# Handing out GpSimd's work on a group of first products two places later, in a kernel of top-k attention and a two-layer block

## The chip, the cores and the metric

The kernel runs on one core of one Trainium2 chip. The metric is the device time of one execution in microseconds; a median of several runs is given for each kernel, and one further execution was recorded by the profiler. The engines are named as in the profile: PE is TensorE, PEld its weight loads, DVE is VectorE, ACT is ScalarE, POOL is GpSimd, SP is SyncE, which issues the DMAs.

## The reference

Attention with the 32 largest scores of each row kept, for 8 batches, 8 heads, 576 positions, 64 values a head; its output is laid out as 4608 rows of 512 and goes through two matrix products with an activation between them.

```python
scores = scale * np.matmul(q, k.transpose(0, 1, 3, 2))
kth = np.partition(scores, -top_k, axis=-1)[..., -top_k:-top_k + 1]
scores = np.where(scores >= kth, scores, -1000000000.0)
attn = np.exp(scores - np.max(scores, axis=-1, keepdims=True))
attn = attn / (np.sum(attn, axis=-1, keepdims=True) + 1e-09)
x = np.matmul(attn, v)                       # (B,H,S,D) -> (B*S, H*D)
h = x @ w_in                                 # 4608 x 512 @ 512 x 2048
g = np.where(h >= 1, h, np.where(h <= -1, 0.0, (h + 1) ** 2 / 4))
out = g @ w_out                              # 2048 x 512
```

All inputs and outputs are 32-bit floats.

## The kernel before, in words

**Steps.** The attention is cut into 144 steps. A step is one tile of 128 rows of one batch for a pair of heads; the 64 rows left over of two batches are paired into steps of their own. The main loop (L744) has index m; each pass is cut into seven places (`SLOTS`, L767), and at each place the loop issues a part of several stages that belong to different steps:

- `scores` (L340): PE multiplies queries and keys (L358), ACT copies the products from PSUM to the tile s (L359). This runs two to three steps ahead.
- `first_top` and `weights` (L382, L417): DVE finds the 32nd largest score of each row. It folds each row into halves (L372, one instruction for the larger and one for the smaller of two elements), and then alternates between taking eight largest (L392, L420, L428, L439) and replacing them (L379); L446 and the scan L451 settle the threshold kth from two sorted lists. ACT makes the exponentials e (L395), and L458 on DVE masks e by the threshold and sums it into z. L372, L451 and L458 are DVE's instructions with two tensors from SBUF.
- `divide` (L402), called inside `weights` of the next step, at its place 0: DVE takes the reciprocal of z (L404), and GpSimd multiplies the two heads' e by it (L411, two instructions), followed by a tiny subtraction for a later check (L414). In the first steps and the last ones (`by_tensor`, L766) a diagonal matrix on PE does the multiplication instead.
- `move_w` (L484), at place 3: ACT copies e to 16-bit halves (L488), which go to DRAM and come back transposed through two DMAs of SP's queue.
- `values` (L498), every two steps: PE multiplies the transposed weights by v (L506), ACT copies the result into a column of xT (L519).

**The two products.** As soon as all heads of 128 rows (a chunk, 36 in all) are in xT, `mlp` (L530) puts this chunk's work on the list `pending`. The 2048 hidden columns are 16 blocks of 128, taken two at a time: a group. `hidden(x)` makes group x: 16 matmul instructions (L539) into a PSUM tile ph, then ACT reads ph twice, as relu of half the value plus a half into r (L543) and as relu of the value minus one into g (L550), and GpSimd does the rest in three instructions: it bounds r at 1 (L555), squares it (L556) and adds it to g (L557). `final(f)` multiplies one block of g by w_out into py (L562), and after 16 blocks ACT copies py to y (L565) and SP stores it. In the list, the two `final` of a group come four groups (`LAG`) behind its `hidden`. r has two buffers and g has eight. For the last chunk, groups are one block wide and DVE takes the place of GpSimd.

**What sets the order.** PE, DVE, ACT and POOL get their instructions in an order written out by hand (`manual_schedule`, L658): the order in which the Python code calls them is the order of each engine's queue. `advance` (L649), called at the end of each place, adds a share to `due` and takes work from `pending` while enough is due: a `hidden` of a group costs 8 units, a `final` 4, and a chunk has 128 units, so that a step is due some 32. `pe_time`, `dve_time` and `usable` are estimates that keep the work from being taken too early. At place 2 of even steps (L795) a `hidden` taken last is followed by further items until a `final` was taken. While the weights are being brought to their form for the products (`converted < n_pieces`, the first eight steps), conversion pieces (L141) use GpSimd too (L158); in this phase a fixed share is due.

So GpSimd's queue holds, in the order of the calls: three instructions for each group, wherever `hidden` was taken, and at place 0 of each step the division L411 (two) with L414.

Of the kernel before, what the change touches and what calls it, by code (L numbers as in the profile page):

```python
# [17 lines left out]
ALU = mybir.AluOpType  # L18
# [8 lines left out]
def kernel(  # L27
# [10 lines left out]
    nc = tc.nc  # L38
# [17 lines left out]
    GROUP = 2  # L56
# [51 lines left out]
    n_pieces = NK * DFF // WC + NF * DM // WC  # L108
# [12 lines left out]
    def needed(f, second):  # L121

        return (f // n_in) * (NK + n_in * n_out) + NK + (n_out * (f % n_in + 1) if second else 0)
# [53 lines left out]
    def run(ctx, paired):  # L177
# [112 lines left out]
        def finish_turns():  # L290
            while turns:
                turns.pop(0)()
# [235 lines left out]
            return [(i * TL, (i + 1) * TL, out[r0 + i * S + SM:r0 + (i + 1) * S, :]) for i in range(2)]  # L528

        def mlp(xT, rows, pool, last):  # L530
            gs, group = {}, 1 if last else GROUP
            py = []

            def hidden(x):
                ph = ps.tile([P, group, P], F32, name="ph", tag="ph", bufs=3)
                for i in range(group):
                    f = x * group + i
                    for kk in range(NK):
                        nc.tensor.matmul(ph[:, i], w_in[:, kk, f * P:(f + 1) * P], xT[:, kk],  # L539
                                         start=(kk == 0), stop=(kk == NK - 1))  # L540

                r = pool.tile([P, GROUP, P], F32, name="r", bufs=2)[:, 0:group]
                nc.scalar.activation(r, ph, AF.Relu, bias=half, scale=0.5 * unit)  # L543
                gs[x] = g = pool.tile([P, GROUP, P], F32, name="g", bufs=2 * LAG)[:, 0:group]
                if last:
                    nc.scalar.activation(g, ph, AF.Relu, bias=minus_half, scale=0.5 * unit)
                    nc.vector.scalar_tensor_tensor(out=r, in0=r, scalar=1.0, in1=r, op0=ALU.min, op1=ALU.mult)
                    nc.vector.tensor_tensor(out=g, in0=r, in1=g, op=ALU.add)
                    return
                nc.scalar.activation(g, ph, AF.Relu, bias=minus, scale=unit)  # L550
                if converted < n_pieces and x % 2:
                    nc.scalar.activation(r, r, AF.Square)
                    nc.gpsimd.tensor_scalar(r, r, 1.0, 0.0, ALU.min, ALU.max)
                else:
                    nc.gpsimd.tensor_scalar(r, r, 1.0, 0.0, ALU.min, ALU.max)  # L555
                    nc.gpsimd.tensor_tensor(out=r, in0=r, in1=r, op=ALU.mult)  # L556
                nc.gpsimd.tensor_tensor(out=g, in0=r, in1=g, op=ALU.add)  # L557

            def final(f):
                if f == 0:  # L560
                    py.append(ps.tile([P, DM], F32, name="py", tag="py", bufs=1))
                nc.tensor.matmul(py[0], gs[f // group][:, f % group], w_out[:, f, :], start=(f == 0), stop=(f == NF - 1))  # L562
                if f == NF - 1:
                    y = (late or words).tile([P, DM], F32, name="y", bufs=1)
                    nc.scalar.activation(y, py[0], AF.Copy, scale=unit)  # L565
                    for p0, p1, dst in rows:
                        nc.sync.dma_start(out=dst, in_=y[p0:p1])

            behind = []
            while pending and pending[-1][3]:
                behind.insert(0, pending.pop())
            for x in range(NF // group + LAG):
                if x < NF // group:
                    pending.append((NK * group, needed(x * group + group - 1, False), partial(hidden, x), False))
                if x < LAG:
                    for _ in range(min(GROUP + 1, len(behind))):
                        pending.append(behind.pop(0)[0:3] + (False,))
                else:  # L580
                    for f in range((x - LAG) * group, (x - LAG + 1) * group):
                        pending.append((DM // P, needed(f, True), partial(final, f), x >= NF // group))
# [14 lines left out]
        n = len(steps)  # L597
# [6 lines left out]
        pending = deque()  # L604
        total, spent = len(chunks) * (NK * NF + NF * DM // P), 0
        converted, inspected, due = 0, 0, 0.0

        begun, pipe = 0, deque()

# [39 lines left out]
        def advance(amount, until):  # L649

            nonlocal due, pe_time
            due = due + amount if pending else 0.0
            pe_time = max(pe_time, until - 4.0)
            while pending and due >= pending[0][0] and pe_time < until and take():
                pass
            due = min(due, 24.0)
# [87 lines left out]
        for m in range(n + 2):  # L744
            early = converted < n_pieces
# [21 lines left out]
            for slot in range(SLOTS):  # L767
                now = start + (dve_time - start) * (slot + 1) / SLOTS
                for _ in range(parts[slot]):
                    next(top_k, None)  # L770
                if m < n and converted < n_pieces:
                    if slot in now_converting:
                        convert(now)
                elif slot == 3 and late is not None:
                    if m % 2:
                        inspect()
                    elif paired:
                        load(late, inspected, 1, 2)
                if slot == 1 and 1 <= m <= n and state[m - 1]["by_tensor"]:
                    pe_time = max(pe_time, done[m - 1] + 2.0) + 1.0  # L780
                    transpose_w(state[m - 1])
                    ready_at[m - 1] = pe_time + 1.8
                if slot == 3 and 1 <= m <= n and state[m - 1] is not None and not state[m - 1]["by_tensor"]:
                    move_w(state[m - 1])
                    ready_at[m - 1] = done[m - 1] + 15.0
                if slot == 3:
                    finish_turns()
                if slot == 2 and m == n and paired:
                    judge(ps, att)
                if slot == 2 and (early or m == first_late or m >= n - 1):  # L790
                    values_until(m)
                if m == 0 and slot in (1, 2):
                    next(first)
                if slot == 2 and not early:
                    if m % 2 == 0:  # L795
                        while pending and taken is not None and taken.__name__ == "hidden" and take():
                            pass
                    begin_until(min(m + 2, len(state)))
                    values_until((m - 2) // 2 * 2)
                    begin_until(m + 3 - m % 2)  # L800
                if slot == 4 and early:
                    begin_at(m + 2)
                if slot == (6 if early else 1):
                    queries(m + (3 if early else 5))
                    if (m < n and prep is None and next_keys < B and steps[m][0] == next_keys - 1 and steps[m][1] >= 1
                            and (next_keys > 1 or converted == n_pieces)):
                        prep = (turned_keys_of if next_keys > 1 else keys_of)(next_keys)
                    if prep is not None and (m % 2 == 0 or next_keys == 1):
                        got = next(prep, None)
                        pe_time += 0.5 if next_keys < 2 else 0.0  # L810
                        if got is None:
                            prep, next_keys = None, next_keys + 1
                        else:
                            keys[next_keys] = got
                            value_loads = got.get("loads", value_loads)
                    elif value_loads is not None:
                        next(value_loads, None)
                if paired and early and spent == 0 and not pending:
                    rest = ps.tile([P, NT, P], F32, name="rest", tag="py", bufs=1)
                    for i in range(5):  # L820
                        nc.tensor.transpose(rest[:, i % NT, :], ident, ident)
                advance((EARLY_SHARE if early else share) / SLOTS if m < n else 32.0, now)
            for _ in (top_k if top_k is not None else ()):
                pass
        while pending:
            advance(32.0, pe_time + 8.0)
        order.__exit__(None, None, None)


# [12 lines left out]
    with ExitStack() as inner:  # L842
        run(inner, True)
# [31 lines left out]
```

## Time and profile before

| | |
|---|---|
| median of 3 runs (lowest, highest) | 1488.8 us (1488.8, 1494.17) |
| the profiled execution, device time | 1492.76 us |
| its span, first to last instruction | 1490.9 us |
| granted TensorE clock, mean | 0.991 |
| instructions | 32088 |
| HBM read and written | 62.91 MB, 102.63 MB |

| POOL's groups | count | mean ns |
|---|---|---|
| L555 bound of r | 276 | 625 |
| L556 square of r | 276 | 730 |
| L557 sum into g | 280 | 789 |
| L411 division of e | 268 | 949 |
| L414 small subtraction | 144 | 462 |

A line of the profile gives a source line, the engine, the operation and the tile that it writes and reads. Means are of single instructions; the time that an instruction is held up after it has begun counts as its own. A bracket at the end of a timeline line is the idle time ahead of the instruction and what ended it. In a line of the waits the numbers are the total, the number of waits and the longest one, in microseconds.

### The profile page before, as it was taken

How to read it: one execution, taken by the hardware profiler on the slowest of the kernel's cores; microseconds unless marked ns; L12 is line 12 of the kernel's file. 1: busy time of each engine (PE TensorE's matmuls, PEld its weight loads, DVE VectorE, ACT ScalarE, POOL GpSimd, SP SyncE). 2: the span in 40 equal slices, each digit the busy share in tenths (PEclk: the TensorE clock that was granted, in tenths of full speed). 3: DMA queues.
4: the chain of work that ended last, by engine and by line, in shares of the span. 5: the costliest groups of instructions: out<-in, count | busy, mean ns of one | idle time of the engine just before them, and what ended most of it. 6: DMA issues, size and time to landing. Idle time of an engine off the chain costs nothing.

```text
span 1490.9 us, 32088 instructions
## 1 busy us (share of the span) xinstructions
PE 1437.7 (96%) x10755; PEld 1044.0 (70%) x10755; DVE 1411.9 (95%) x4392; ACT 1157.7 (78%) x2221; POOL 949.8 (64%) x1310
## 2 busy tenths in 40 slices
PE   7998899999999999999999999999999999999998
PEld 5765677777777777677767776767777777777675
DVE  6989999999999999999999999999999999999912
ACT  7986877888788877787778888788778887777632
POOL 3474576666676666666766667666666666677730
PEclk8999999999999999999999999999999999999999
DMA  8533567766677777886667786887677876665400
GB/s 253 193 120 107 149 170 203 198 182 170 170 202 197 192 184 204 204 209 177 170 186 199 198 200 173 208 214 182 170 201 187 203 202 168 161 167 138 149 25 17
DMA packets 510319, 260.94 MB, mean 175 GB/s; under 512 B 460992, under 2 KB 469184, under 8 KB 510144
## 3 DMA queue, kind: packets, MB, share of 16 engines
q1 hardware_dynamic: 510144, 258.80, 66.0%
q8 instruction: 87, 1.43, 0.4%
q14 instruction: 88, 0.72, 0.2%
HBM read 62.91 MB, written 102.63 MB: 111 GB/s over the span
## 4 chain that ended last, share of the span: by engine, by line
PE 65%; DVE 13%; ACT 10%; DMA 5%; POOL 4%; issue 3%; SPq 0%; POOLq 0%; ACTq 0%; DVEq 0%
PE py L562 26%; PE ph L539 23%; PE sp L358 8%; PE po L506 6%; DVE more L379 3%; ACT halves L488 2%; DVE e L458 2%; DMA rows<-halves 2%; ACT e L395 2%; POOL r L556 2%; DMA wT<-rows 2%; ACT r L543 1%; DVE more L372 1%; POOL g L557 1%; DVE tops L420 1%
## 5 line engine op out<-in xcount | busy, mean ns | idle before, releaser
L539 PEld LDWEIGHTS ph<-xT,w_in 128*128 128x128 f32 x4608 | 547.1, 192 | 102.3 <-issue 78.6
L539 PE MATMUL ph<-xT,w_in 128*128 128x128 f32 x4608 | 555.6, 276 | 2.3 <-ACT g L550 1.4
L562 PE MATMUL py<-w_out,g 128*128 128x512 f32 x1152 | 542.3, 597 | 0.7 <-ACT y L565 0.7
L555 POOL TENSOR_SCALAR r<-r 128x256 f32<-128x256 f32 x276 | 172.4, 625 | 401.3 <-ACT r L543 401.3
L379 DVE MATCH_REPLACE8 more<-tops,more 128x288 f32<-128x288 f32 x864 | 375.0, 437 | 0.0
L562 PEld LDWEIGHTS py<-w_out,g 128*128 128x128 f32 x1152 | 199.5, 191 | 165.1 <-issue 159.8
L488 ACT COPY halves<-e 128x1152 uint16<-128x1152 uint16 x268 | 293.7, 1143 | 19.9 <-DMA rows<-halves 12.5
L411 POOL TENSOR_SCALAR e<-e,rz 128x576 f32<-128x576 f32 x268 | 251.6, 949 | 10.0 <-DVE rz L404 10.0
L458 DVE SCALAR_TENSOR_TENSOR e<-s,kth,e 128x577 f32<-128x577 f32 x288 | 252.5, 912 | 0.5 <-ACT e L395 0.4
L543 ACT ACTIVATE r<-ph,half 128x256 f32<-128x256 f32 (+1 forms) x296 | 135.9, 459 | 145.2 <-PE ph L539 101.5
L557 POOL TENSOR_TENSOR g<-r,g 128x256 f32<-128x256 f32 x280 | 221.0, 789 | 22.0
L395 ACT ACTIVATE e<-s,nmax 128x576 f32<-128x576 f32 x288 | 222.6, 773 | 4.7
L556 POOL TENSOR_TENSOR r<-r 128x256 f32<-128x256 f32 x276 | 201.6, 730 | 23.0
L359 ACT ACTIVATE s<-sp 128x576 f32<-128x576 f32 x288 | 171.6, 649 | 52.6 <-PE sp L358 51.7
L358 PE MATMUL sp<-kT,qT 64*128 64x288 f32 x1024 | 163.9, 438 | 18.0 <-ACT s L359 12.4
L358 PEld LDWEIGHTS sp<-kT,qT 64*128 64x128 f32 x1024 | 89.0, 189 | 91.7 <-issue 35.3
L506 PE MATMUL po<-wT,v_in 128*64 128x128 f32 x2048 | 138.3, 276 | 6.4 <-DMA wT<-rows 5.6
L506 PEld LDWEIGHTS po<-wT,v_in 128*64 128x64 f32 x2048 | 113.2, 137 | 30.7 <-issue 11.4
L372 DVE TENSOR_TENSOR more<-s 128x576 f32<-128x576 f32 x144 | 122.5, 850 | 8.3 <-ACT s L359 8.3
L550 ACT ACTIVATE g<-ph,minus 128x256 f32<-128x256 f32 x280 | 129.8, 464 | 0.0
L420 DVE MAX8 tops<-more 128x8 f32<-128x288 f32 x288 | 125.4, 443 | 0.0
L392 DVE MAX8 tops<-more 128x8 f32<-128x288 f32 x288 | 116.4, 443 | 0.0
(92 smaller groups left out, 1378.3 us busy)
## 6 DMA issues: line engine op xcount, KB each, us to landing
rows<-halves SPq DMA_DIRECT2D x134, 576.0 KB, 3.4
lines<-parts SPq DMA_DIRECT2D x48, 256.0 KB, 2.7
q_in<-in_q_dram SPq DMA_DIRECT2D x32, 256.0 KB, 3.9
v_in<-in_v_dram SPq DMA_DIRECT2D x32, 256.0 KB, 4.3
out_dram<-y SPq DMA_DIRECT2D x32, 256.0 KB, 4.1
raw<-in_moe_w_in_dram SPq DMA_DIRECT2D x32, 256.0 KB, 3.3
raw<-in_moe_w_out_dram SPq DMA_DIRECT2D x32, 256.0 KB, 3.5
kT<-in_moe_w_in_dram SPq DMA_DIRECT2D x8, 512.0 KB, 4.8
```

The source lines that it names most:

```text
L358: nc.tensor.matmul(*x, start=True, stop=True)
L379: nc.vector.match_replace(out=st["rest"][:, i, :], in_to_replace=eight(st["tops"], i, r - 8), in_values=src[:, i, :], imm_value=LOWEST)
L395: nc.scalar.activation(e[:, i, :], s[:, i, :], AF.Exp, bias=nmax[:, i:i + 1])
L411: nc.gpsimd.tensor_scalar(st["e"][:, i, :], st["e"][:, i, :], rz[:, i:i + 1], 1.0, ALU.mult, ALU.mult)
L458: nc.vector.scalar_tensor_tensor(out=st["all"][1][:, i, :], in0=st["all"][0][:, i, :], scalar=last[i], in1=st["all"][1][:, i, :], op0=ALU. ...
L488: nc.scalar.copy(halves[:, :, i * S:(i + 1) * S], st["e"][:, i, :].bitcast(U16).rearrange("p (k t) -> p t k", t=2))
L506: nc.tensor.matmul(po[j * D:(j + 1) * D], v_in[:, h, c, :] if c < NT else v_tl[0][:, h, :], wT[:, block(j, c)], start=(c == 0), stop=(c == ...
L539: nc.tensor.matmul(ph[:, i], w_in[:, kk, f * P:(f + 1) * P], xT[:, kk], start=(kk == 0), stop=(kk == NK - 1))
L555: nc.gpsimd.tensor_scalar(r, r, 1.0, 0.0, ALU.min, ALU.max)
L556: nc.gpsimd.tensor_tensor(out=r, in0=r, in1=r, op=ALU.mult)
L557: nc.gpsimd.tensor_tensor(out=g, in0=r, in1=g, op=ALU.add)
L562: nc.tensor.matmul(py[0], gs[f // group][:, f % group], w_out[:, f, :], start=(f == 0), stop=(f == NF - 1))
```

## The change

`hidden(x)` is cut in three. `hidden` itself issues the matmuls and queues `read`, which is called at once, since `holding` is never set. `read` issues ACT's two instructions as before and, in place of issuing GpSimd's, appends `bound` to the queue `bounds`, with the number of places passed so far (`slots_done`). `bound` issues GpSimd's three instructions. It is called

- at the end of a place, once more than two places lie behind the group's own, so at the end of the second place after it; at the end of the group's own place while weights are converted and in the passes after the last step;
- at the start of a later `read`, if two groups are still queued;
- in `final`, if that needs a group not yet handed out.

The last chunk's groups, which DVE makes, are not queued. The first three instructions and the two of the form with ACT's square (L551 to L553) are the same in number and operands.

```diff
         def mlp(xT, rows, pool, last):
-            gs, group = {}, 1 if last else GROUP
+            gs, group, whole_g = {}, 1 if last else GROUP, set()
...
+                reads.append(partial(read, x, ph))
+                if not holding:
+                    issue_reads()
+
+            def read(x, ph):
+                while len(bounds) > 1:
+                    bounds.popleft()[1]()
                 r = pool.tile([P, GROUP, P], F32, name="r", bufs=2)[:, 0:group]
                 nc.scalar.activation(r, ph, AF.Relu, bias=half, scale=0.5 * unit)
...
                 nc.scalar.activation(g, ph, AF.Relu, bias=minus, scale=unit)
-                if converted < n_pieces and x % 2:
+                by_act = converted < n_pieces and x % 2
+                if by_act:
                     nc.scalar.activation(r, r, AF.Square)
-                    nc.gpsimd.tensor_scalar(r, r, 1.0, 0.0, ALU.min, ALU.max)
-                else:
-                    nc.gpsimd.tensor_scalar(r, r, 1.0, 0.0, ALU.min, ALU.max)
+                bounds.append((slots_done, partial(bound, x, r, g, by_act)))
+
+            def bound(x, r, g, by_act):
+                nc.gpsimd.tensor_scalar(r, r, 1.0, 0.0, ALU.min, ALU.max)
+                if not by_act:
                     nc.gpsimd.tensor_tensor(out=r, in0=r, in1=r, op=ALU.mult)
                 nc.gpsimd.tensor_tensor(out=g, in0=r, in1=g, op=ALU.add)
+                whole_g.add(x)
 
             def final(f):
...
+                if f // group not in gs:
+                    issue_reads()
+                while f // group not in whole_g:
+                    bounds.popleft()[1]()
                 nc.tensor.matmul(py[0], gs[f // group][:, f % group], w_out[:, f, :], ...)
...
+        reads, bounds, holding, slots_done = [], deque(), False, 0
...
                 advance((EARLY_SHARE if early else share) / SLOTS if m < n else 32.0, now)
+                slots_done += 1
+                while bounds and (early or m >= n or bounds[0][0] < slots_done - 2):
+                    bounds.popleft()[1]()
```

More of the change, by code (lines that the diff above doesn't have):

```diff
@@ L548, in hidden @@
                     nc.vector.tensor_tensor(out=g, in0=r, in1=g, op=ALU.add)
+                    whole_g.add(x)
                     return
                 nc.scalar.activation(g, ph, AF.Relu, bias=minus, scale=unit)
-                if converted < n_pieces and x % 2:
+                by_act = converted < n_pieces and x % 2
+                if by_act:
                     nc.scalar.activation(r, r, AF.Square)
-                    nc.gpsimd.tensor_scalar(r, r, 1.0, 0.0, ALU.min, ALU.max)
-                else:
-                    nc.gpsimd.tensor_scalar(r, r, 1.0, 0.0, ALU.min, ALU.max)
+                bounds.append((slots_done, partial(bound, x, r, g, by_act)))
+            def bound(x, r, g, by_act):
+                nc.gpsimd.tensor_scalar(r, r, 1.0, 0.0, ALU.min, ALU.max)
+                if not by_act:
                     nc.gpsimd.tensor_tensor(out=r, in0=r, in1=r, op=ALU.mult)
                 nc.gpsimd.tensor_tensor(out=g, in0=r, in1=g, op=ALU.add)
+                whole_g.add(x)
             def final(f):
@@ L606, in run, with issue_reads @@
         converted, inspected, due = 0, 0, 0.0
+        reads, bounds, holding, slots_done = [], deque(), False, 0
+        def issue_reads():
+            while reads:
+                reads.pop(0)()
         begun, pipe = 0, deque()
@@ L826, in run @@
             advance(32.0, pe_time + 8.0)
+            while bounds:
+                bounds.popleft()[1]()
         order.__exit__(None, None, None)
```

## The prediction

> **What bounds the kernel now.** I read the page's busy line first, then a table of busy time by stretch, then the waits, then the timeline of single steps (a step is one pass of the loop at L744: 144 of them, each 128 rows of two heads).
>
> ```profile
> PE 1437.7 (96%) x10755; PEld 1044.0 (70%) x10755; DVE 1411.9 (95%) x4392; ACT 1157.7 (78%) x2221; POOL 949.8 (64%) x1310
> ```
>
> Two engines are nearly full. The table (length, then busy us of PE, PEld, DVE, ACT, POOL) shows where each has slack:
>
> ```profile
> 600.00:1000.00 400.00, 391.68 (x2979) 282.03 (x2979) 400.00 (x1242) 322.99 (x612) 270.53 (x369) 1.00 0.76 194
> 1000.00:1200.00 200.00, 200.00 (x1451) 145.47 (x1452) 200.00 (x637) 163.76 (x314) 132.37 (x193) 1.00 0.77 191
> 1440.00:1491.00 51.00, 44.36 (x227) 29.68 (x225) 9.37 (x32) 13.71 (x40) 5.21 (x9) 0.97 0.04 13
> ```
>
> From 200 to 1400 us DVE is never idle; PE is idle 14.7 us of those 1200, and it alone works through the last 51. So the end is PE's, and before it the two run side by side, DVE with no wait at all. The waits, all engines in the whole span, then PE's between 200 and 1400:
>
> ```profile
> POOL r L555 <- ACT r L543: 401.3, 124, 9.9
> POOL e L411 <- DVE rz L404: 10.0, 1, 10.0
> ```
>
> ```profile
> PE sp L358 <- ACT s L359: 10.4, 16, 1.4
> ```
>
> GpSimd waits for ScalarE's relu, and the division (L411) waits for the reciprocal once only: it is always kept by what stands before it in its queue. Over steps 21 to 140 it starts 4.5 to 7.6 us after the reciprocal, by the step's number modulo 4: 7.6 (0), 6.2 (1), 4.5 (2), 4.7 (3). Now one step with number 76, so 0 modulo 4:
>
> ```profile
> 772.92 0.14 DVE L404 RECIPROCAL rz<-z 128x2 f32<-128x2 f32 x1
> ...
> 775.42 0.40 POOL L555 TENSOR_SCALAR r<-r 128x256 f32<-128x256 f32 x1 [4.16 <-ACT r L543]
> ...
> 775.90 1.74 POOL L556 TENSOR_TENSOR r<-r 128x256 f32<-128x256 f32 x1
> ...
> 777.72 0.73 POOL L557 TENSOR_TENSOR g<-r,g 128x256 f32<-128x256 f32 x1
> ...
> 778.42 0.40 POOL L555 TENSOR_SCALAR r<-r 128x256 f32<-128x256 f32 x1
> ...
> 779.59 0.73 POOL L557 TENSOR_TENSOR g<-r,g 128x256 f32<-128x256 f32 x1
> 779.68 0.70 DVE L451 TENSOR_TENSOR_SCAN kth<-tops,seconds 128x25 f32<-128x25 f32 x1
> ...
> 780.30 1.97 POOL L411 TENSOR_SCALAR e<-e,rz 128x576 f32<-128x576 f32 x2
> ...
> 780.72 0.93 DVE L458 SCALAR_TENSOR_TENSOR e<-s,kth,e 128x577 f32<-128x577 f32 x1
> ...
> 781.58 1.29 DVE L458 SCALAR_TENSOR_TENSOR e<-s,kth,e 128x577 f32<-128x577 f32 x1
> ```
>
> And a step with number 1 modulo 4, where the division starts 5.9 us after the reciprocal:
>
> ```profile
> 744.58 0.14 DVE L404 RECIPROCAL rz<-z 128x2 f32<-128x2 f32 x1
> ...
> 750.58 1.50 POOL L411 TENSOR_SCALAR e<-e,rz 128x576 f32<-128x576 f32 x2
> ...
> 751.91 0.81 DVE L458 SCALAR_TENSOR_TENSOR e<-s,kth,e 128x577 f32<-128x577 f32 x1
> ...
> 752.64 0.81 DVE L458 SCALAR_TENSOR_TENSOR e<-s,kth,e 128x577 f32<-128x577 f32 x1
> ...
> 753.75 0.14 DVE L404 RECIPROCAL rz<-z 128x2 f32<-128x2 f32 x1
> ```
>
> The second step takes DVE 9.17 us (744.58 to 753.75), the first 10.25 (772.92 to 783.17). The difference lies in three DVE instructions: the scan 0.70 against 0.23, the maskings 0.93 and 1.29 against 0.81 twice. All three stand beside GpSimd's L557 and L411.
>
> **What the Trainium skill says.** "SBUF — State Buffer", section "SBUF: two separate sides": DVE and GpSimd share one pair of ports under an exclusive lock, taken by a DVE instruction with two SBUF inputs against a GpSimd instruction that reads SBUF; whoever starts first keeps it to its end. The trace agrees: L458 takes 0.81 us alone and up to 1.29, L556 0.61 and up to 1.74 (above, across both L372). "Perfetto Trace Analysis", section "Sequencer Loop": an instruction goes into its engine's queue and waits there for its semaphores; the trace agrees, since the division stands behind groups whose relu isn't there yet. The head of the same page calls matmul busy time a bad metric; so I take PE's 100% as "no visible wait" only.
>
> **The change, part by part.** What ScalarE, TensorE, VectorE and the DMA queues get, and in which order, is the same: only L555 to L557 (1.74 us a group when not blocked: 0.40+0.61+0.73) change place in GpSimd's own queue, past L411 and L414. No instruction and no semaphore wait is added.
>
> *How many move.* A step has seven places; a group taken at place p is handed out at the end of p+2, the next division at place 0 of the next step. So only groups taken at places 5 and 6 come behind it; the many at place 4 are handed out at place 6, still ahead. Following the planner's own numbers (costs of 8 and 4 units, 32 units a step), the places repeat every four steps: 1,4 | 1,4 | 3 | 0,4,6. One group in eight is at 6. Over the run **33 of 280 groups** move, each past one division, all but one in steps 0 modulo 4 from 12 to 140. While weights are converted, and past the last step, groups are handed out at once.
>
> *What it costs the group.* It ends some 3 us later (at 783.3 instead of 780.3 in the step shown). Who waits: the relu two groups on, for its buffer, at 785.5 there, so 2.2 us of cover; and matmuls L562 four groups, some 19 us, behind. Cost nothing; without that cover 1 us per moved group at most on ScalarE, 33 us, which I exclude as the gap is visible in the repeating pattern.
>
> *What it gives the division.* It starts about 1.9 us earlier in those steps (778.42 instead of 780.30). ScalarE's copy L488 starts at 782.72, straight after another ScalarE instruction: it gains nothing. The gain is in DVE's lock. I sort the 33 steps by how long the division now waits:
>
> - 6.8 to 7.4 us, 16 steps, mostly 10.25 us long, so about 1.1 over the 9.14 of a free step. After: division at about 5.4. The pair L411 then meets only the scan's start (step 110 has this: scan 0.28, +0.09); behind it comes the moved group and meets the maskings. Step 35 shows that order (division, then a group at once): its maskings take 0.83 and 1.28, +0.49. Bounds 0.49 and 0.70 (both, and 0.12 on the first masking); I take 0.6. Gain 0.5 x 16 = 8.0 us.
> - 7.7 to 8.0 us, 8 steps of 10.09 on average. After: 5.8 to 6.1, the pattern of step 73 above, which also has L414 and a group behind it: 9.17. Gain 0.92 x 8 = 7.4 us. Bound from below: 0.
> - 5.9 to 6.6 us, 4 steps: the group takes the division's place on the maskings; 0.
> - 8.5 us and more, 5 steps of 9.67 on average: now the division falls behind the maskings; after, at 6.6 to 7, it falls upon them. Loss 0 to 0.6, I take 0.3 x 5 = 1.5 us.
>
> DVE sum: 8.0 + 7.4 - 1.5 = 13.9 us less.
>
> *How much reaches the end.* PE must follow. In 14 of the 16 steps of the first kind PE waits for s (L358, the row above; 0.69 us in most, 0.2 to 0.4 in four), because ScalarE waits for a group that DVE's L372 blocks. If DVE comes 0.5 us sooner against PE, PE's wait shrinks by as much, or to nothing: 10 x 0.5 + 1.3 = 6.3 us. In the second kind's stretches (309 to 358, 1080 to 1193) PE shows 100%, and DVE only gets ahead; that is worth about 1 us of the 4.0 that PE waits after 1400, and, since a busy PE may hide waits (309 to 358 takes 9.64 us a step, 1080 to 1193 9.43, both at 100%), I let a quarter of the 7.4 through, 1.7. Sum **-9 us**. Against the profiled execution (span 1490.9, 1492.8 with the 1.9 around it): 1483.8. The median shown, 1488.8, is 4.0 lower, so I take 9 from that: **1480**.
>
> **The rivals.**
> 1. *Nothing reaches the end.* PE's wait hangs on a group that isn't moved (L557 at 777.72 is before both), and DVE is never PE's visible releaser. DVE gains and stands ahead, PE takes its time: 0 to -4 us, 1487. For it: PE 100% in whole stretches. Against it: PE's wait repeats at 0.69 from step to step of this kind while both engines show the same 38.6 us for four steps, so one holds the other. A variant: 33 moved groups of 280 are too few to be seen; the same time.
> 2. *Slower: the division now meets the maskings.* With a start later than about 6.1 us after the reciprocal, L411's 1.47 us run past 7.2, where L458 begins; then scan, L458 and L458 pay 0.26, 0.48 and 0.61, 1.35 in all, and the group behind adds another L557, 0.3. That is 1.65 against 0.5 in steps now above 8.5 us. Should a faster DVE slide the phase there in half of the 33 steps: 16 x 1.1 = 18 us, two thirds of it on PE: +12, 1501. For it: 5 steps are there already. Against: PE's wait pulls the phase back.
> 3. *The ceiling.* Steps 104 to 120 take 37.85 us per four with PE at 100%; the mean of steps 20 to 140 is 38.42. Were all at 37.85: 0.57 x 31 = -17.7, 1471.
>
> **How the numbers follow.** A change can be told from none here at about 0.5%, 7.4 us, so from 1481.4 to 1496.2. Forecast 48% (own range 1475 to 1485, about 10 of the 48 above 1481.4), rival 1 27%, rival 2 15%, rival 3 10%. Faster 38+10 = 48%, same 10+27 = 37%, slower 15%. The range reaches from 1472, which leaves out half of rival 3 (5%), to 1494, which leaves out most of rival 2 (13%).
>
> **What would show it.** Right: in steps 0 modulo 4 L411 starts 5.3 to 6.1 us after the reciprocal, a whole group stands behind it, the scan is back to 0.3, the mean step there falls from 10.06 to about 9.6, the other three kinds stay near 9.39, 9.48 and 9.50; PE's wait for s falls from 10.4 to about 4 us. Wrong: L411 as late as before (an earlier group holds it), the two maskings as long as before beside the moved group, other steps growing, or DVE quicker and the end where it was.

## The result and the profile after

| | before | after |
|---|---|---|
| median | 1491.87 us (8 runs, 1488.8 to 1494.17) | 1483.43 us (8 runs, 1482.35 to 1486.89) |
| profiled execution: span | 1490.9 us | 1480.7 us |
| mean wait of L411 behind the reciprocal, steps 0 modulo 4 | 7.6 us | 6.4 us |

The ratio is 0.995 (95% interval 0.9936 to 0.9964): 8.4 us less between the medians. The forecast was 9 us less and 1480, counted from another median of before (1488.8, three runs). In the changed kernel, source lines 543, 550, 555, 556, 557 and 562 are 550, 558, 565, 567, 568 and 578.

The page's busy line after the change:

```profile
PE 1436.5 (97%) x10755; PEld 1044.2 (71%) x10755; DVE 1401.9 (95%) x4392; ACT 1157.7 (78%) x2221; POOL 918.4 (62%) x1310
```

The work is the same to the instruction, yet DVE is busy 10.0 us less and GpSimd 31.4: both busy times hold the time in which an instruction stands still after it has begun, and the two stand in each other's way less. DVE's alone says little of the cause: it is idle only near the start and the end, so its busy time goes down with the span (10.2 us less). L411's mean goes from 949 to 842 ns. The table by stretch (columns as in the prediction):

```profile
600.00:1000.00 400.00, 395.95 (x3022) 287.90 (x3021) 400.00 (x1259) 326.99 (x620) 267.44 (x375) 1.00 0.77 197
1000.00:1200.00 200.00, 200.00 (x1452) 144.25 (x1451) 200.00 (x633) 164.68 (x316) 133.09 (x192) 1.00 0.78 189
1440.00:1481.00 41.00, 34.74 (x175) 22.92 (x173) 9.35 (x32) 11.23 (x34) 0.69 (x1) 0.97 0.04 16
```

PE is idle 7.4 us between 200 and 1400 us, where it was 14.7; DVE is never idle there, as before. The waits of the whole span after the change, ScalarE's of them before, and then PE's between 200 and 1400 after it:

```profile
POOL r L565 <- ACT r L550: 420.4, 139, 8.6
...
ACT r L550 <- POOL g L568: 24.8, 24, 2.0
...
POOL e L411 <- DVE rz L404: 10.0, 1, 10.0
```

```profile
ACT r L543 <- POOL g L557: 40.1, 28, 3.8
```

```profile
PE sp L358 <- ACT s L359: 3.5, 6, 1.1
```

The division still never waits for its reciprocal but once, so a group is still ahead of it in nearly every step. In this execution much of PE's wait for s has gone (10.4 before), and much of ScalarE's wait for GpSimd's sum (40.1 before, 24.8 after): the relu L550 needs a buffer of r, and the sum two groups earlier is the last to use it. I call this ScalarE's wait for r. A step 0 modulo 4 of the changed kernel, number 112:

```profile
1110.65 0.14 DVE L404 RECIPROCAL rz<-z 128x2 f32<-128x2 f32 x1
...
1114.76 0.40 POOL L565 TENSOR_SCALAR r<-r 128x256 f32<-128x256 f32 x1 [2.65 <-ACT r L550]
...
1115.93 0.73 POOL L568 TENSOR_TENSOR g<-r,g 128x256 f32<-128x256 f32 x1
...
1116.64 1.50 POOL L411 TENSOR_SCALAR e<-e,rz 128x576 f32<-128x576 f32 x2
...
1117.41 0.22 DVE L451 TENSOR_TENSOR_SCAN kth<-tops,seconds 128x25 f32<-128x25 f32 x1
...
1117.96 0.80 DVE L458 SCALAR_TENSOR_TENSOR e<-s,kth,e 128x577 f32<-128x577 f32 x1
...
1118.70 0.81 DVE L458 SCALAR_TENSOR_TENSOR e<-s,kth,e 128x577 f32<-128x577 f32 x1
...
1118.80 0.97 POOL L565 TENSOR_SCALAR r<-r 128x256 f32<-128x256 f32 x1
...
1119.82 0.14 DVE L404 RECIPROCAL rz<-z 128x2 f32<-128x2 f32 x1
```

One group stands before L411 and one behind it (L565 at 1118.80), the scan and both maskings have their free lengths, and the step takes 9.17 us from reciprocal to reciprocal. Over steps 21 to 139 the means of the four kinds of step are (0, 1, 2, 3 modulo 4), worked out from the reciprocals of the timeline:

| | 0 | 1 | 2 | 3 | four steps |
|---|---|---|---|---|---|
| before | 10.06 | 9.39 | 9.48 | 9.50 | 38.43 |
| after | 9.45 | 9.83 | 9.52 | 9.31 | 38.12 |

So the moved steps gained 0.6 us each, and the steps behind them gave half of it back. That was the question for the experiments: which engine sets the pace, and through what does the moved group reach the end?

### The profile page after: what moved, and what is told of

Its sections match the earlier page's. It is cut to its first block, busy times and chain, and to the rows that moved or that the text cites. A ratio compares the mean times of both kernels' runs of the same rounds, so it can differ in the third digit from the quotient of the medians.

```text
span 1480.7 us, 32120 instructions
## 1 busy us (share of the span) xinstructions
PE 1436.5 (97%) x10755; PEld 1044.2 (71%) x10755; DVE 1401.9 (95%) x4392; ACT 1157.7 (78%) x2221; POOL 918.4 (62%) x1310
## 4 chain that ended last, share of the span: by engine, by line
PE 83%; ACT 5%; DMA 5%; DVE 2%; issue 2%; POOL 1%; SPq 1%; POOLq 0%; ACTq 0%; DVEq 0%
PE ph L539 31%; PE py L578 31%; PE sp L358 10%; PE po L506 9%; DMA rows<-halves 2%; DMA wT<-rows 2%; ACT halves L488 1%; ACT e L395 1%; PE po L514 1%; PE pw L473 1%; ACT r L550 1%; ACT s L359 1%; DVE more L379 0%; DVE bits L156 0%; POOL g L568 0%
## 5 line engine op out<-in xcount | busy, mean ns | idle before, releaser
L565 POOL TENSOR_SCALAR r<-r 128x256 f32<-128x256 f32 x280 | 177.5, 634 | 424.0 <-ACT r L550 420.4
L458 DVE SCALAR_TENSOR_TENSOR e<-s,kth,e 128x577 f32<-128x577 f32 x288 | 249.2, 900 | 0.1
L550 ACT ACTIVATE r<-ph,half 128x256 f32<-128x256 f32 (+1 forms) x296 | 136.1, 460 | 128.0 <-PE ph L539 101.8
L411 POOL TENSOR_SCALAR e<-e,rz 128x576 f32<-128x576 f32 x268 | 222.9, 842 | 10.0 <-DVE rz L404 10.0
L567 POOL TENSOR_TENSOR r<-r 128x256 f32<-128x256 f32 x276 | 187.6, 680 | 23.0
L372 DVE TENSOR_TENSOR more<-s 128x576 f32<-128x576 f32 x144 | 120.5, 837 | 7.4 <-ACT s L359 7.4
L392 DVE MAX8 tops<-more 128x8 f32<-128x288 f32 x288 | 116.5, 443 | 0.0
```

The lines of the kernel that those rows point to most:

```text
L411: nc.gpsimd.tensor_scalar(st["e"][:, i, :], st["e"][:, i, :], rz[:, i:i + 1], 1.0, ALU.mult, ALU.mult)
L458: nc.vector.scalar_tensor_tensor(out=st["all"][1][:, i, :], in0=st["all"][0][:, i, :], scalar=last[i], in1=st["all"][1][:, i, :], op0=ALU. ...
```

## The experiments

**Theory A**, as predicted: DVE's collisions with GpSimd set the pace, PE's wait for s shrinks because DVE comes sooner. **Rivals**: the weights reach PE earlier; moving anything merely shuffles collisions; or PE's own wait behind ScalarE is the cause and DVE only follows. The table gives all runs. PE's idle time is that between 200 and 1400 us of the profiled execution (1200 less PE's busy time there), and the wait for r is ScalarE's for GpSimd's sum in the same stretch.

| run | ratio to before (95%) | wait for r | PE idle | DVE busy | span |
|---|---|---|---|---|---|
| before | 1 | 36.1 | 14.7 | 1411.9 | 1490.9 |
| after | 0.995 (0.9936 to 0.9964) | 22.3 | 7.4 | 1401.9 | 1480.7 |
| one place later | 0.9974 (0.9963 to 0.9984) | 33.6 | 13.5 | 1409.0 | 1487.2 |
| three places later | 1.0021 (0.9997 to 1.0044) | 42.8 | 22.0 | 1422.1 | 1499.4 |
| no division | 0.9953 (0.9938 to 0.9968) | 32.6 | 13.2 | 1409.5 | 1488.0 |
| before, three r | 0.9941 (0.9922 to 0.996) | 0 | 6.0 | 1403.5 | 1481.8 |
| after, three r | 0.9922 (0.9904 to 0.9941) | 0 | 5.1 | 1398.5 | 1478.2 |
| three places, three r | 1.003 (1.0017 to 1.0043) | 0 | 14.9 | 1415.6 | 1494.1 |
| before, lighter DVE | 0.9986 (0.9975 to 0.9997) | 32.1 | 9.2 | 1361.6 | 1485.0 |
| after, again | 0.9954 (0.9937 to 0.997) | 35.0 | 13.0 | 1406.6 | 1488.4 |
| late steps only | 0.9997 (0.9979 to 1.0015) | 34.6 | 12.3 | 1408.3 | 1490.1 |
| early steps only | 0.9949 (0.9934 to 0.9965) | 25.4 | 8.7 | 1404.4 | 1484.5 |
| three places, three r, lighter DVE | 0.9914 (0.9884 to 0.9944) | 0 | 6.3 | 1356.0 | 1479.7 |
| after, three r, lighter DVE | 0.9921 (0.9894 to 0.9948) | 0 | 5.7 | 1385.9 | 1476.9 |

Read down the columns: in the profiled executions the span goes with PE's idle time (5 to 7.4 us of it: spans of 1477 to 1482; 8.7 and 9.2: 1485; 12 to 15: 1487 to 1494; 22: 1499), and, where r has two buffers and DVE its full work, both go with the wait for r (22.3 and 25.4 have the two shortest spans). DVE's busy time goes with the span as well, 77 to 82 us below it in every run with DVE's full work, since it is idle only at the ends. Only the three runs with a lighter DVE can tell the two engines apart (1361.6 us go with 1485.0, 1398.5 with 1478.2).

### One place later

```diff
-                while bounds and (early or m >= n or bounds[0][0] < slots_done - 2):
+                while bounds and (early or m >= n or bounds[0][0] < slots_done - 1):
```

> Groups are handed out one place later instead of two. In GpSimd's queue 32 of the 33 moved groups then stand exactly where the changed kernel has them, since a group taken at place 6 comes behind the division in both; one group, of step 9, stays ahead. Theory A (all that counts is that the group taken at place 6 gets behind the division of the next step): as the changed kernel, ratio to before 0.993 to 0.997, and PE's wait for s at L358 between 200 and 1400 us near 3.5 us. Theory B (the size of the delay counts): half the gain, 0.997 to 0.999.

Measured 0.9974, in theory B's range, and PE's wait for s was 10.2 us: theory A missed both its numbers, the ratio by little. GpSimd's queue differs from the changed kernel's by one group, that of step 9. The changed kernel itself, run again on another chip, settled how to take this.

### The changed kernel again

> The changed kernel once more, for the same chip as the three others: 0.993 to 0.997 by every theory. Of interest is how far single runs spread, since the kernel with one place later differs from it by the place of one group in step 9 and gave 0.9974.

Measured 0.9954, with single runs from 1481.94 to 1490.22; the profiled one was the longest of them, with PE idle for 13.0 us. In that execution PE's wait for s was 9.8 us and ScalarE's for r 35.0, nearly those of before. So one kernel can run with 7.4 or with 13.0 us of PE idle time, and the intervals of "one place later" and of this run overlap. The place of step 9's group was not shown to matter.

### Three places later

```diff
-                while bounds and (early or m >= n or bounds[0][0] < slots_done - 2):
+                while bounds and (early or m >= n or bounds[0][0] < slots_done - 3):
```

> Three places later: the groups taken at place 4 get behind the division too, some 120 of 280. Theory A (the gain is DVE's, from fewer collisions with GpSimd, and what reaches the end is limited by PE's own waits, of which 7.4 us are left in the changed kernel between 200 and 1400 us): the division starts within 1 us of its reciprocal in three steps of four, DVE's busy time falls by 10 to 25 us more, the end by at most 7 us more: ratio to before 0.989 to 0.995. Theory B (the gain came from the weights that reach PE earlier): the division comes 5 us earlier still in three times as many steps, so three times the gain, 0.985. Theory C (moving anything merely shuffles the collisions): 0.995 to 1.005.

Measured 1.0021; single runs lie between 1481 and 1503, and four of the 22 below 1484, as short as the changed kernel's. The division starts 0.1 us after the reciprocal in three steps of four, 4 to 8 us earlier than before, and the end is no earlier. That refutes the rival of the earlier weights. Theory A missed too: in the profiled execution, one of the long ones, DVE was busier by 10 us, and PE waited more. The number is in theory C's range.

### The division left out

```diff
                 for i in range(2):
-                    nc.gpsimd.tensor_scalar(st["e"][:, i, :], st["e"][:, i, :], rz[:, i:i + 1], 1.0, ALU.mult, ALU.mult)
+                    pass
```

> The kernel before with L411 left out: the weights of 134 steps are not divided by their sum, so its output is another. Nothing else changes. Theory A (what counts is that GpSimd's instructions hold up DVE's two-input ones, and PE is the next bound): DVE's busy time falls by 20 us or more and the end by 10 to 18 us, ratio 0.988 to 0.993, no more, since PE's own work stays. Theory B (the end hangs on PE alone and DVE's collisions cost nothing): 0.998 to 1.0.

Measured 0.9953, between the theories, and no more than the change gives by moving 33 groups past it. DVE's busy time fell by 2.4 us where 20 were expected; but the profiled execution was the longest of eight (1489.8, median 1484.6). With 252 us of GpSimd's work gone, DVE met the remaining groups instead: the scan's mean rose from 289 to 332 ns and that of GpSimd's sum from 789 to 846, while the maskings' fell from 912 to 902 only. So DVE's collisions are no fixed sum that goes with the instructions. ScalarE's wait for r (32.6 us) and PE's for s (10.4) were still there.

### Three buffers of r

```diff
-                r = pool.tile([P, GROUP, P], F32, name="r", bufs=2)[:, 0:group]
+                r = pool.tile([P, GROUP, P], F32, name="r", bufs=3)[:, 0:group]
...
-                gs[x] = g = pool.tile([P, GROUP, P], F32, name="g", bufs=2 * LAG)[:, 0:group]
+                gs[x] = g = pool.tile([P, GROUP, P], F32, name="g", bufs=2 * LAG - 1)[:, 0:group]
```

The same edit was made in the kernel before, in the changed kernel, and in that with three places (g gives up one buffer for r's third).

> The kernel before with three buffers of r and seven of g instead of two and eight. ScalarE no longer waits for GpSimd's L557 of two groups before (43 us in all), so PE's wait for s at L358 (10.4 us between 200 and 1400) goes. Queue orders stay. Theory A (DVE sets the pace in the steps where PE waits): the wait moves elsewhere, DVE's busy time stays within 3 us, ratio 0.997 to 1.0. Theory B (PE sets the pace and this wait is what costs): the 10 us come off the end, ratio 0.993.

Measured 0.9941: theory B. No group moves here, and the whole gain of the change is there. PE's wait for s between 200 and 1400 us:

```profile
PE sp L358 <- ACT s L359: 1.3, 2, 1.0
```

DVE's busy time fell by 8.4 us, although nothing of its own or of GpSimd's was touched. By itself this doesn't say which engine leads, since the buffer changes when DVE and GpSimd meet, too; the runs with a lighter DVE do, below.

> The changed kernel with three buffers of r and seven of g, as the run with three buffers of r did it to the kernel before. Theory A (the change works through one wait, ScalarE's relu on GpSimd's sum two groups before, and through that PE's wait for s): with a third buffer that wait is gone already, so the change adds nothing: ratio 0.993 to 0.996, as with three buffers alone (0.994). Theory B (the change works through DVE's collisions, apart from that wait): both gains add, 0.988 to 0.991.

Measured 0.9922, below the bounds of theory A and above those of theory B, with an interval that overlaps that of three buffers alone. Were the two gains apart, 0.9941 x 0.995 = 0.989 was to be expected. So most of what the change gives is gone once the wait is gone; whether the last 0.2% is real stays open.

> Three places later, with three buffers of r and seven of g. Three places alone gave 1.002, from 1481 to 1503 us. Theory A (what three places lose is lost in ScalarE's wait for r's buffer): 0.992 to 0.996 and a spread no wider than of the kernel before. Theory B (what they lose is lost in DVE's collisions with the moved groups): 1.000 to 1.004 again.

Measured 1.003: theory B. ScalarE now waits for DVE's first eight largest, which are L392 (between 200 and 1400 us; 0.5 us in the kernel before):

```profile
ACT nmax L393 <- DVE tops L392: 116.5, 76, 3.2
```

The row alone doesn't prove that DVE sets the pace: with three buffers in the kernel before it is 61.8 us, and there the end came sooner.

### DVE made lighter

```diff
             for x in largest(st, 16):
                 x()
-            for i in range(2):
+            for i in range(1):
                 replace(st, 24, i)
```

> The kernel before with one of the six replacements of a step left out (L379 for the second head in the last round), so the threshold of that head is another: DVE has 144 x 0.43 = 62 us less to do. Theory A (DVE sets the pace of the steps in which PE waits): the end falls by 10 to 18 us, down to PE's own work, 0.988 to 0.993, and DVE begins to wait for s. Theory B (PE sets the pace, and its wait for s comes from a meeting of GpSimd's L556 with DVE's L372 at a certain phase): the end moves by less than 5 us either way, or becomes longer if the phase of the meeting lasts.

Measured 0.9986: 50 us less DVE busy time, 2 us off the end. Theory B, though DVE does begin to wait for s, as theory A had it. DVE and ScalarE in that run, 200 to 1400 us:

```profile
ACT r L543 <- POOL g L557: 32.1, 28, 2.0
```

```profile
DVE e L458 <- ACT e L395: 24.8, 37, 1.4
DVE more L372 <- ACT s L359: 11.9, 14, 1.4
```

DVE, never idle before, now waits, and ScalarE's wait for r's buffer is still there (36.1 us in the same stretch before).

> Three places later with three buffers of r (1.003), and with one of DVE's six replacements of a step left out, 62 us in all; the threshold of the second head is another. Theory A (with r's wait gone, that kernel is paced by DVE, which GpSimd's groups hold up behind the division; ScalarE waited 116 us for DVE's first eight largest there): the end falls to PE's own work, ratio 0.988 to 0.993. Theory B (what it loses is lost between GpSimd, ScalarE and PE): 1.000 to 1.004 again.

Measured 0.9914: theory A. In the order with three places, alone of the three that were tried with a lighter DVE, DVE does set the pace: taking 62 us off it brings 1.003 to 0.9914, and ScalarE's wait for DVE's L392 is no longer among its waits.

> The changed kernel with three buffers of r (0.9922), and with the same replacement left out. Theory A (little is left that DVE holds up there: ScalarE waited 26 us for DVE): 0.988 to 0.992, the ceiling that PE's own work sets, about 1472 us. Theory B (DVE still sets the pace there): below 0.985.

Measured 0.9921, the same as without the lighter DVE, 1479.5 us: at the edge of theory A's range and clear of theory B's. With r's wait gone and the group moved, DVE's work no longer limits the end. The end expected from PE's own work, 1472 us, was not reached, and PE is still idle for 5.7 us there. What DVE did with the time is in its maskings, without the lighter DVE and with it:

```profile
L458 DVE SCALAR_TENSOR_TENSOR e<-s,kth,e 128x577 f32<-128x577 f32 x288 | 239.4, 867 | 0.1
```

```profile
L458 DVE SCALAR_TENSOR_TENSOR e<-s,kth,e 128x577 f32<-128x577 f32 x288 | 276.5, 992 | 7.1 <-ACT e L395 7.0
```

Some 61 us of replacements are gone, but DVE's busy time fell by 12.6 us only: the same maskings take 37 us more, the scan 10.

**Whose pace it is.** Where a run repeats a pattern, four steps take the following times (from the reciprocals of the timeline):

| run | steps | four steps | PE idle in them |
|---|---|---|---|
| after | 104 to 124 | 37.77 | 0 |
| before, three r | 112 to 120 | 37.77 | 0 |
| before, lighter DVE | 68 to 80 | 37.77 | 0 |
| after, three r, lighter DVE | 132 to 140 | 37.77 | 0 |
| three places, three r, lighter DVE | 104 to 120 | 37.77 | 0 |
| before, lighter DVE | 104 to 120 | 38.26 | 0.36 |
| after, again | 68 to 88 | 38.42 | 0.53 |
| before | 72 to 88 | 38.58 | 0.69 |
| before, three r | 28 to 44 | 38.23 | 0 to 0.2 |
| three places, three r | 104 to 124 | 38.40 | 0 to 1.1 |

The same 37.77 comes back whether the group is moved or not, and whether DVE has its full work or 1.7 us less in four steps (61/36): so it isn't DVE that sets it, and PE is never idle in it. The next three rows lie above it by PE's wait and 0.1 more. The last two lie above it without such a wait. In the last, the time stays while PE's changes, and it comes down to 37.77 with the lighter DVE: there DVE sets the pace. What holds "before, three r" from step 28 to 44 was not settled.

### Early and late steps

```diff
-                while bounds and (early or m >= n or bounds[0][0] < slots_done - 2):
+                while bounds and (early or m < 100 or m >= n or bounds[0][0] < slots_done - 2):
```

> The change from step 100 on only: 10 of the 33 groups move. In the traces so far, steps 124 to 140 take 151 us in the changed kernel and its two relatives and 154.6 before, and steps 12 to 124 differ by 0 to 6.7 us between runs of the same kernel. Theory A (the gain is that the last steps keep a pattern in which PE doesn't wait): about -3.5 us, ratio 0.9965 to 0.9985, with PE's waits after 1200 us gone. Theory B (each moved group gives the same): 10/33 of the gain, 0.9985.

The other half has `m >= 100` in the place of `m >= n`.

> The change up to step 99 only: 23 of the 33 groups move. Theory A: the rest of the gain, -1 to -5 us, 0.9965 to 0.9995, with PE's waits for s after 1200 us as before. Theory B: 23/33 of the gain, 0.9965 to 0.997.

Measured 0.9997 and 0.9949. By the medians the late groups alone give nothing and the early ones all, so theory A missed; but the intervals reach to 0.9979 and to 0.9965, so equal shares (0.9985, and 0.9965 to 0.997) are not excluded. The start of the reciprocal of steps 36, 92 and 140, from the timelines:

| | 36 | 92 | 140 | from 36 to 92 |
|---|---|---|---|---|
| before | 387.2 | 927.1 | 1385.8 | 539.9 |
| late steps only | 388.3 | 929.3 | 1383.7 | 541.0 |
| after | 384.8 | 920.6 | 1375.1 | 535.8 |
| after, again | 388.2 | 925.1 | 1382.0 | 536.9 |
| one place later | 386.4 | 923.6 | 1380.8 | 537.2 |
| early steps only | 383.8 | 920.1 | 1377.3 | 536.3 |

From step 36 to 92 the four executions with 14 groups moved take 3 to 5 us less than the two with none: that part came in each. It isn't all visible as idle time of PE, which is 8.6 us before in these steps, 3.3 in the changed kernel, but 8.3 in its second run and 8.9 with one place later. The rest of the run differs by as much between executions with the same order there: from 92 to 140, "early steps only" has the order of before from step 101 on and takes 457.2 us, before takes 458.7, "late steps only" 454.4.

**What happens from step 36 to 92.** First the kernel before in step 76 again, now by ScalarE and PE:

```profile
774.87 0.45 ACT L543 ACTIVATE r<-ph,half 128x256 f32<-128x256 f32 x1
...
775.76 0.74 DVE L372 TENSOR_TENSOR more<-s 128x576 f32<-128x576 f32 x1
...
778.48 0.47 ACT L543 ACTIVATE r<-ph,half 128x256 f32<-128x256 f32 x1 [2.06 <-POOL g L557]
...
779.91 1.30 PE L358 MATMUL sp<-kT,qT 64*128 64x288 f32 x8 [0.69 <-ACT s L359]
```

The relu of the next step's first group waits for the sum of the group two before (at 777.72 in the prediction's lines), whose square L556 took 1.74 us beside DVE's two L372, and 0.61 in the next group. ScalarE's copies of s queue behind that relu, and PE waits for them. Now the same step in the second run of the changed kernel, which kept this wait:

```profile
775.06 0.45 ACT L550 ACTIVATE r<-ph,half 128x256 f32<-128x256 f32 x1
775.28 0.74 DVE L372 TENSOR_TENSOR more<-s 128x576 f32<-128x576 f32 x1
775.60 1.35 POOL L565 TENSOR_SCALAR r<-r 128x256 f32<-128x256 f32 x1 [4.09 <-ACT r L550]
...
777.73 0.73 POOL L568 TENSOR_TENSOR g<-r,g 128x256 f32<-128x256 f32 x1
778.44 1.55 POOL L411 TENSOR_SCALAR e<-e,rz 128x576 f32<-128x576 f32 x2
778.49 0.47 ACT L550 ACTIVATE r<-ph,half 128x256 f32<-128x256 f32 x1 [1.90 <-POOL g L568]
...
779.92 1.30 PE L358 MATMUL sp<-kT,qT 64*128 64x288 f32 x8 [0.53 <-ACT s L359]
```

The relu stands 0.67 us later against DVE: it comes 0.22 us ahead of L372, and before 0.89 (774.87 against 775.76). It is the first of the group's three instructions that is held, not the second, and the sum follows the relu by 3.4 us, not 3.6. PE's wait falls from 0.69 to 0.53 each four steps. In the first run of the changed kernel steps 64 to 80 have no such wait at all, although from step 68 to 80 the division starts 7.4 us after the reciprocal, no sooner than before (7.1 and 7.2), and still meets the maskings (0.86 and 1.29 us in step 76). The second run has the earlier division (5.9) and the wait. So it is not the earlier division that takes PE's wait away. Both patterns repeat for twelve steps and more. Which of them a run falls into, and what throws it from one into the other, was not settled.

## Why the prediction was right, and where it was not

- *How many move*: right. In GpSimd's queues of the two kernels, laid side by side, 33 groups change place against a division, all but one in steps 0 modulo 4.
- *What it costs the group*: right. The cover held: ScalarE's wait for r over the whole span went from 40.1 to 24.8 us, and to 36.2 in the second run. The case without cover is "three places later", where that wait is 42.8 us between 200 and 1400 (36.1 before) and the gain is gone, though not by this alone.
- *What it gives the division*: right in kind and place for the steps 0 modulo 4. They fell from 10.06 to 9.45; 9.6 was expected. The division starts 1.2 us earlier there (7.6 to 6.4), where 1.9 was forecast: at 5.9 in about half of them, not at the 5.4 that I took for the first kind, and at 7.4 to 7.6 from step 60 to 80. In the other three kinds it starts 1.0 to 1.3 us later than before (7.1, 5.8 and 5.8), which I hadn't foreseen.
- *DVE's sum, -13.9 us*: too large, and the step that failed is that the other three kinds of step stay as they are. They went from 9.39, 9.48 and 9.50 to 9.83, 9.52 and 9.31. With some 30 steps of each kind the first gain is 0.61 x 30 = 18 us, of which 0.29 x 30 = 9 went back; DVE's busy time fell by 10.0.
- *How much reaches the end*: the sum was right (9 forecast, 8.4 measured), and PE's wait for s was the right row (10.4 to 3.5 us, "about 4" expected). The reason given was wrong, so that the sum came out is luck in part: DVE's gain was taken too large, and the way to the end was another. I wrote that PE's wait shrinks because DVE comes sooner. In the second run PE's wait for s was 9.8, so the forecast of about 4 holds for one of two executions. DVE with 50 us less to do brought 2 us; a third buffer of r, with DVE's work untouched, brought 8.8 (0.0059 x 1490.6). PE's pace includes ScalarE's wait for r, and DVE, which shows no wait, follows PE: where it gets ahead, its instructions with two tensors from SBUF meet other GpSimd instructions and take longer (the maskings' 867 and 992 ns above).
- *Rival 1* spoke for PE as the pace and was right in that; the group on which PE's wait hangs isn't moved, as it says, but its wait changed all the same (0.69, 0.53 or none in step 76). *Rival 2*, collisions behind an order that is too late, is what the order with three places shows once r has a third buffer. *Rival 3* had the pace right (37.85 for four steps, 37.77 in the table above) and the end wrong: no run kept it throughout, and 1479 is what is left with r's wait and some of DVE's load both taken away.
- What stays open: the run that was profiled for the result is among the better ones of its kernel. The part that came back in each of four executions is 3 to 5 us from step 36 to 92; for the rest of the 8 us only the medians speak. And how a group moved past the division shortens ScalarE's wait for r was read in one step, not shown for the run.

The best version tried that computes the same output is the changed kernel with three buffers of r: 1479.7 us, 0.9922 of before. Its interval overlaps that of three buffers alone (0.9941).

## What to carry to other kernels

An engine without a single wait can still be the one that follows: when its instructions are held up by another engine's, as DVE's by GpSimd's here, its busy time can stretch to fill the time that the pace leaves. Take load off it and see whether the end moves, before its busy time is priced. Look for a ring of buffers with little depth between the engines that do show waits (here r, two deep, between ScalarE and GpSimd): one more buffer did what a finer order of the queue did (0.9941 and 0.995).

## What the runs showed that I had not expected

Leaving 252 us of GpSimd's work out took 2.4 us off DVE's busy time in a long execution, and adding a buffer took 8.4 off it. A kernel with fixed queues settled for sixteen to twenty steps into a repeating pattern of four steps, of 38.6 us (before, steps 72 to 88) or 37.8 (after, steps 104 to 124), and two executions of the changed kernel chose differently from step 68 to 80 (37.8 and 38.4).
